# GpSimd takes the six products of C and B, seven column steps move to the front, three PSUM copies change engine, and the order list is new

## The chip, the cores and the metric
The kernel runs on one core of a Trainium2 chip. The metric is the device time of one execution in microseconds (us). The kernel before was timed three times: 318.88, 318.61 and 317.36 us, median 318.61 us. A core has five engines that run side by side, each strictly in its own order: TensorE (PE, with its weight loads shown as PEld), VectorE (DVE), ScalarE (ACT), GpSimd (POOL) and SyncE (SP), which here only issues transfers.

## The reference, cut to what matters
The input x (2048 rows, 640 channels) goes through two branches, and a gate mixes them.

```python
g = sigmoid((x * gate_w).sum(-1, keepdims=True))
# a: per channel d a long convolution with K[d, l], over N = 128 modes
dt = exp(log_dt)[:, None]
logdA, dB = dt * (A_re + 1j*A_im), dt * (B_re + 1j*B_im)
P = exp(logdA[:, :, None] * l)
K = einsum("dn,dnl,dn->dl", C_re + 1j*C_im, P, dB).real
a = irfft(rfft(x, 2L) * rfft(K, 2L))[:L] + x * Dskip
# b: a gated feed-forward block, F = 1728
b = (gelu(x @ w_gate) * (x @ w_up)) @ w_down
return g * a + (1 - g) * b
```

The part that changes is at the start. The product C times B is complex; its real part `vr` = Cre·Bre − Cim·Bim and its imaginary part `vi` = Cre·Bim + Cim·Bre are turned into a size and an angle, from which the tables for K are built.

## The kernel before
Everything is unrolled in Python. The list `ORDER` sets the order of the work: each word is one step, its first letter the kind, digits the indices, and a last letter A or D says whether ScalarE or VectorE does a copy. A planner then places each engine's instructions at compile time by its own reckoning of time, and takes a later step early where the engine would be idle in that reckoning. Chains of dependences keep some of it fixed: `first()` ties VectorE's early steps together in program order, and `table()` does so for most ScalarE steps. Copies of PSUM made by `copy()` (L127 on ScalarE, L131 on VectorE) are in neither chain.

The steps that matter here:
- `a` (`scaled_a`): dt is spread over the partitions by TensorE, ScalarE takes its exponential (`dtb`, L336), VectorE multiplies (`a32`, `b32`, L349 to L351).
- `M` (`early_phases`, L508): VectorE writes phases of the transform matrices. It runs twice.
- `i0` (`columns`, L304 to L319): eleven VectorE steps on columns of one to five elements, in the `first` chain, then seven small GpSimd fills. `i1` makes the flip matrices, `i2` GpSimd's fills (helper L283).
- `x` (`turn_x`): TensorE transposes four or eight 128x128 tiles of x into a PSUM buffer named `cv` (L255), and VectorE (D, L260) or ScalarE (A, L258) copies them to `xT`. `x00` to `x02` make the 640 channels of rows 0 to 511 (c = 0), `x10` to `x12` those of rows 512 to 1023 (c = 1). There are two `cv` buffers, taken in turn, and `x1*` needs the second input transfer.
- `u` (`ffn_up`, L632): ten matmuls of 128x512 into one of two `gu` buffers, gate and up of one feature tile; `pA` or `pD` copies it to `GU` (L127 or L131), `o` sends it to DRAM on SP's queue. There are 56 such steps, and they fill TensorE between other work up to some 165 us. The first four are two of c = 0 and two of c = 1.
- `v` (`phase_and_size`, L439 to L447): the six VectorE products and sums for `vr` and `vi`, 128x640 each, in the `first` chain. Ahead of them stand GpSimd's fill of `zero` and two small GpSimd transfers (`dskc`, `gwc`).
- `S0`, `S1` (`squares` on ScalarE, `sizes` on VectorE), then `r0`, `r1`, `r2`: square root, half angle, angle. `e..` (`exps`, L385) are the exponentials of the tables on ScalarE.
- `t` (`trig`): VectorE writes phases `ph` (L413 and L417, L421), ScalarE takes the sine (L429). `q` (`ktable`, L582 to L590) multiplies the tables on VectorE.
- `!0` (`turn_over(0)`): four GpSimd transfers write `zero` into `GUd` (L913), then the memory of the first stage is given to the tables of `q`.

Of the kernel before, what the change touches and what calls it, by code (L numbers as in the profile page):

```python
# [38 lines left out]
e10 pA u u o e11 e14 t05 y4 pA u t07 u !0 pA pA o pA q05 u u u pA pA o o W o pA o o t02 pA t06 q07 u u q06 y0 t00 pA  # L39
t01 t03 pD o q01 q00 o y1 o o W u pA o q02 q04 u q03 pD t14 o u c02 t10 t16 u pA o c00 pD u C00A c10 pD c01 u !1 pA W  # L40
o o q10 u C01D C02A C10A m u c11 C11D w0 u o pA pA c12 m o u C12A W w1 pA m u pA u o o t11 pA q11 o W u t17 t15 e24 pA
u o pD u o u o pD u pA o W o pD u pD q15 W o e23 pA e22 o u e25 q16 q17 u e20 pD e21 u o o pD o pA t13 o t12 q12 m q14
m u q13 c20 c22 pA C20A u c21 C21D t20 c30 m m c32 !2 pA u C30A t21 C32A c31 m C22A f0 m w2 C31A o t22 q20 F0P t23 U00
U03 U01 V01A w3 V00A q22 q23 pD o U02 h K00 u V03A pA K02 Q00D Q02D o q21 K03 u K01 V02A Q01D Q03A c40 f1 pA C40A o !3
W b00 F1P l00 G00 u L0 c41 C41D pA c42 o l01 C42A l10 g00 b01 w4 f2 U10 b10 b11 P00D U12 P01D V10A u P02D U13 V12A pA
u pA o K10 o K12 Q12A Q10A P03D U11 u G01 K11 V13A pA L1 V11A F2A K13 Q13A Q11A K20 g01 D00 D01 Q20A P10D K22 K21 Q21A
d01A U20 U22 Q22A V20A P11D d00A l11 V22A l20 U23 V23A o K23 D02 f3 Q23A d02D G10 g10 F3A I00 U21 U30 P12D V30A U33
D03 G11 V21A o P20D U31 D10 I10 V33D d10A V31A f4 U32 D11 b20 z00D d03A g11 d11A D13 K30 d13A I01 V32A F4A Q30A K32
Q32A K31 P21D z10A D12 l21 P22D b21 Z00A G20 d12A P23D Q31A l30 Z01A g20 D20 K42 U40 G21 z01A K40 P13D d20D I11 g21
V40A z11A Q40A K41 b30 G30 D21 I20 U42 D23 Q41A K33 d23D K43 d21A Q33A l31 Q43M P30D D22 d22A Z02A Q42A g30 U41 P31D  # L50
b31 D30 V41D I21 G31 V42A U43 z20D V43D d30D g31 z21A P40D D32 P32D P33D d32A I30 z30A D31 J33 j33D d31A D33 J32 d33A
Z03A P41D Z11A P42D J41 J40 j41A P43D j40A j32A Z12A Z10A Z20D J43 J42 j43D Z21D j42A Z22M Z23D Z13D
"""


# [1 line left out]
def kernel(  # L57
# [18 lines left out]
    nc = tc.nc  # L76
    Bsz, L, D = A_u.shape
    N = A_A_re.shape[1]
# [4 lines left out]
    NFULL = F // 128  # L83
    FR = F - 128 * NFULL
    assert 2 * FR == 128
    DP = 128
# [20 lines left out]
    def load_set(x):  # L107
        table(nc.scalar.add_instruction(mybir.InstLoadActFuncSet(
            name=nc.get_next_instruction_name(), engine=mybir.EngineType.Activation, act_func_set_id=x)))

    last_first = [None]
# [164 lines left out]
    def ts(out, in0, s1, s2, op0, op1=None):  # L276
        if op1 is None:
            first(nc.vector.tensor_scalar(out=out, in0=in0, scalar1=s1, scalar2=s2, op0=op0))
        else:
            first(nc.vector.tensor_scalar(out=out, in0=in0, scalar1=s1, scalar2=s2, op0=op0, op1=op1))  # L280

    def fill(out, v):
        nc.gpsimd.memset(out, v)  # L283

    def fills():
        for q, vals in ((0, (3, 1, 3, 1)), (1, (5, 3, 5, 3))):
# [14 lines left out]
            fill(c2[r:r + 1, 6:7], float(c2v))  # L301
        fill(KTt[:, 5], 0.0)

    def columns():  # L304
        first(nc.vector.tensor_copy(out=row[:], in_=par_i[:]))
# [131 lines left out]
    va, vb, vr, vi = (pw.tile([N, D], FP32, name=x) for x in ("va", "vb", "vr", "vi"))  # L437

    def phase_and_size():  # L439
        nc.gpsimd.memset(zero[:], 0.0)  # L440
        nc.gpsimd.dma_start(out=dskc[:], in_=A_Dskip.rearrange("(k p) -> p k", p=128))
        nc.gpsimd.dma_start(out=gwc[:], in_=gate_w.rearrange("(k p) -> p k", p=128))
        for dst, (x0, y0, x1, y1), op in ((vr, (CreT, BreT, CimT, BimT), ALU.subtract),
                                          (vi, (CreT, BimT, CimT, BreT), ALU.add)):
            first(tt(out=va[:], in0=x0[:], in1=y0[:], op=ALU.mult))
            first(tt(out=vb[:], in0=x1[:], in1=y1[:], op=ALU.mult))
            first(tt(out=dst[:], in0=va[:], in1=vb[:], op=op))  # L447

    def squares():
        table(nc.scalar.activation(out=va[:], in_=vr[:], func=ACT.Square))  # L450
# [75 lines left out]

    def early_phases():
        k = 4 + 2 * len(early)
        early.append(phases_of(mats[len(early)], DFT[:, k:k + 2].rearrange("p a r f -> p (a r f)").bitcast(I32)))

    def dft_matrix(mi):
        if mi >= 6:
# [376 lines left out]
    def turn_over(x):  # L909

        if x == 0:
            for c in range(4):
                nc.gpsimd.dma_start(out=GUd[c][FR:128, NFULL], in_=zero[FR:128])  # L913
            ictx.__exit__(None, None, None)
            pools["kq"] = pool(ectx, "kq")
        elif x == 1:
            bctx.__exit__(None, None, None)
            kb4 = pool(kctx, "ktab4", side="right")
            tabs[2] = (kb4.tile([N, 1, NA, DP], BF16, name="eA4"), kb4.tile([N, 1, GP, NB_, 4], BF16, name="eB4"))
        elif x == 2:  # L920
            ectx.__exit__(None, None, None)
            es = pool(ctx, "early")
            pools["mp"] = pool(ctx, "prod")
            pools["kq"] = pool(kctx, "kq4", side="right")
            pools.update(ub=es, pm=es, spec=es)
# [25 lines left out]
    for step in ORDER.split():  # L951
# [5 lines left out]
        if kind == "u" and ups[0][0] < 2:  # L957
            after(*(f"x{ups[0][0]}{i}" for i in range(3)))
        elif kind == "u":
            after(*(f"y{k}" for k in range(KT_)))  # L960
        elif kind == "M":
            assert len(mats) == NMAT + 1 and len(early) < 3
        elif kind == "m":
            after("s", *(("i0", "i2") if len(mats) <= NMAT - 3 else ()), *(("n", "k") if len(mats) <= 5 else ()))
        elif kind in "lb":
            assert not made and all(p[0] != x for p in ups + unsent)
        elif kind == "!" and x == 0:
            assert len(mats) <= NMAT - 1
            after("k", "i0", "i1", "i2", "r2")
# [141 lines left out]
```

## Time and profile before
| | |
|---|---|
| median of three runs | 318.61 us |
| the profiled execution: time | 319.25 us |
| its span | 317.1 us |
| PE busy | 294.0 us (93%) |
| DVE busy | 296.2 us (93%) |
| ACT busy | 246.9 us (78%) |
| POOL busy | 14.2 us (4%) |

The profiled execution took 319.25 us, of which the span from its first to its last record is 317.1 us. The engines' busy times are unions over time: a matmul that overlaps the next counts once. In a timeline row the columns are start, duration (of a whole group where several instructions are merged), engine, line, operation, the tiles as out<-in with shapes, and the count; in square brackets stands how long the engine had been idle before and what ended that. A row of the windows view gives the busy time of each engine in a stretch.

### The profile page before, as it was taken

The numbers are of one execution on the slowest core, as the hardware profiler recorded it, in microseconds if no ns is written. First come the engines' busy times: TensorE is split into PE (matmuls) and PEld (weight loads), VectorE is DVE, ScalarE is ACT, GpSimd is POOL, SyncE is SP. The second block draws the span as 40 slices with busy tenths as digits, with TensorE's granted clock in tenths as the row PEclk, the third lists the DMA queues.
The fourth block names the chain that finished last, engine by engine and source line by source line (L and its number), as shares of the span: only waits on it lengthen the run. The fifth ranks groups of instructions, "written<-read, shape, count | busy, mean of one in ns | idle before, by whom it ended". The sixth has DMA issues, their size and how long they took to land.

```text
span 317.1 us, 6300 instructions
## 1 busy us (share of the span) xinstructions
PE 294.0 (93%) x2463; PEld 182.0 (57%) x2463; DVE 296.2 (93%) x417; ACT 246.9 (78%) x349; POOL 14.2 (4%) x78
## 2 busy tenths in 40 slices
PE   3499999999999999999998879999999999999994
PEld 2344444444555344454476567666686887687773
DVE  4887989999998999999999999989999999999984
ACT  7979999999898999998998667927696737542750
POOL 7720000000000000000000000000000000000000
PEclk9999999999999999999999999999999999999999
DMA  7997456566628885544594699946925352900233
GB/s 214 182 257 193 168 184 207 182 194 216 182 70 178 210 276 179 150 110 128 103 270 151 118 317 236 234 116 168 244 74 165 89 151 63 265 2 0 58 95 83
DMA packets 102543, 51.40 MB, mean 162 GB/s; under 512 B 44081, under 2 KB 95730, under 8 KB 102514
## 3 DMA queue, kind: packets, MB, share of 16 engines
q1 hardware_dynamic: 102256, 50.48, 59.8%
q0 software_dynamic: 256, 0.53, 0.6%
q8 instruction: 19, 0.31, 0.4%
q14 instruction: 10, 0.08, 0.1%
q10 hardware_dynamic: 2, 0.00, 0.0%
HBM read 30.86 MB, written 18.16 MB: 155 GB/s over the span
## 4 chain that ended last, share of the span: by engine, by line
PE 47%; DVE 22%; ACT 14%; DMA 8%; issue 5%; SPq 2%; DVEq 0%; ACTq 0%
PE gu L794 15%; PE gu L632 8%; PE cv L869 6%; DVE ph L413 5%; PE cv L735 4%; PE cv L718 4%; DMA Wd<-in_B_w_down_dram 3%; ACT eA L385 2%; ACT eB L385 2%; PE cv L893 2%; DMA T<-in_A_u_dram 2%; DMA Kd<-Kraw 2%; DVE ph L421 2%; DVE eB L590 1%; DVE sB L589 1%
## 5 line engine op out<-in xcount | busy, mean ns | idle before, releaser
L632 PE MATMUL gu<-xT,W 128*128 128x512 bf16 x540 | 123.7, 383 | 2.8 <-ACT GU L127 1.7
L632 PEld LDWEIGHTS <-W 128*128 128x128 bf16 x540 | 52.3, 99 | 70.1 <-issue 12.5
L794 PE MATMUL gu<-Wd,HT 128*128 128x320 bf16 x448 | 64.4, 299 | 1.1 <-DMA Wd<-in_B_w_down_dram 1.1
L794 PEld LDWEIGHTS <-HT 128*128 128x128 bf16 x448 | 43.5, 98 | 19.2 <-issue 1.3
L429 ACT ACTIVATE T<-ph 128x1024 bf16<-128x1024 int16 (+3 forms) x40 | 46.3, 1196 | 2.6 <-DVE ph L413 1.5
L127 ACT CAST GU<-gu 128x1024 bf16<-128x1024 f32 (+1 forms) x33 | 32.2, 981 | 4.6 <-PE gu L632 3.2
L813 DVE TENSOR_TENSOR Tp<-Uf,Kf 128x6144 bf16<-128x6144 bf16 (+2 forms) x15 | 34.3, 2287 | 0.1
L778 ACT ACTIVATE HT<-HT 128x1792 bf16<-128x1792 bf16 x16 | 26.5, 1692 | 7.0 <-DMA HT<-GUd 5.5
L818 DVE TENSOR_TENSOR Mb<-Mb,Tp 128x4096 bf16<-128x4096 bf16 (+1 forms) x15 | 29.0, 1933 | 0.2
L131 DVE CAST GU<-gu 128x1024 bf16<-128x1024 f32 (+1 forms) x23 | 27.0, 1174 | 0.5 <-PE gu L632 0.5
L735 PE MATMUL cv<-KTt,DFT 128*128 128x128 bf16 x280 | 24.2, 219 | 0.6 <-ACT Uf L127 0.3
L129 ACT ACTIVATE ob<-gu,rat 128x640 bf16<-128x640 f32 x12 | 9.5, 795 | 18.3 <-PE gu L794 18.3
L385 ACT ACTIVATE eB<-a 128x256 bf16<-128x256 f32 (+2 forms) x63 | 23.3, 451 | 0.0
L735 PEld LDWEIGHTS <-DFT 128*128 128x128 bf16 x280 | 21.0, 98 | 1.2 <-issue 0.4
L718 PE MATMUL cv<-pm,DFT 128*128 128x512 bf16 x80 | 20.1, 378 | 1.3 <-DVE Kraw L133 0.6
L127 ACT CAST Uf<-cv 128x1024 bf16<-128x1024 f32 x17 | 16.9, 1019 | 5.2 <-PE cv L718 3.2
L129 ACT ACTIVATE Kf<-cv 128x512 bf16<-128x512 f32 x33 | 17.6, 597 | 3.8 <-PE cv L735 3.7
L413 DVE SCALAR_TENSOR_TENSOR ph<-b,phi 128x256 int32<-128x256 f32 (+1 forms) x63 | 19.6, 385 | 0.0
L869 PEld LDWEIGHTS <-DFT 128*128 128x128 bf16 x320 | 18.8, 98 | 1.3 <-DVE HT L133 0.3
L735 PE MATMUL cv<-KTt,ME 128*128 128x128 bf16 x120 | 18.6, 219 | 0.0
L783 DVE TENSOR_TENSOR HT<-HT,Ut 128x1792 bf16<-128x1792 bf16 x16 | 17.1, 1086 | 0.1
L385 ACT ACTIVATE eA<-a 128x256 bf16<-128x256 f32 (+2 forms) x42 | 15.2, 444 | 0.9 <-DVE a L349 0.9
(182 smaller groups left out, 455.0 us busy)
## 6 DMA issues: line engine op xcount, KB each, us to landing
GUd<-GU SPq DMA_DIRECT2D x52, 256.0 KB, 2.3
HT<-GUd SPq DMA_DIRECT2D x16, 448.0 KB, 4.7
Ut<-GUd SPq DMA_DIRECT2D x16, 448.0 KB, 4.8
W<-in_B_w_gate_dram SPq DMA_DIRECT2D x12, 320.0 KB, 3.5
W<-in_B_w_up_dram SPq DMA_DIRECT2D x12, 320.0 KB, 4.3
fo<-in_A_u_dram SPq DMA_DIRECT2D x20, 128.0 KB, 3.0
out_dram<-GU SPq DMA_DIRECT2D x8, 256.0 KB, 2.6
T<-in_A_u_dram SPq DMA_DIRECT2D x2, 640.0 KB, 7.5
```

The costliest lines, as they stand in the source:

```text
L127: nc.scalar.copy(out=dst, in_=src)
L129: nc.scalar.activation(out=dst, in_=src, func=ACT.Copy, scale=scale)
L385: table(nc.scalar.activation(out=dst, in_=src, func=ACT.Exp, scale=float(scale)))
L413: nc.vector.scalar_tensor_tensor(out=ph[:, x, :], in0=b32[:, dsl], scalar=float(A_OF[x0 + x] + MID), in1=phi[:, dsl], op0=ALU.mult, op1=AL ...
L429: table(nc.scalar.activation(out=dst, in_=phl, func=ACT.Sin, scale=-SIN_SCALE if r and x1 > NA else SIN_SCALE))
L632: nc.tensor.matmul(p[:, r], lhsT=W[:, kt, f0:f0 + 128], rhs=xT[:, kt, 512 * c:512 * (c + 1)], start=(kt == 0), stop=(kt == KT_ - 1))
L718: nc.tensor.matmul(pU[:, ri], lhsT=dmat(e, ri, m), rhs=pm[:, ri, e].rearrange("p c d -> p (c d)"), start=(e == 0), stop=(e == 1))
L735: nc.tensor.matmul(pW[:, ri, 128 * m:128 * (m + 1)], lhsT=lhs, rhs=rhs, start=(first and x == 0 and m == 0), stop=(x == len(seq) - 1), ski ...
L794: nc.tensor.matmul(pD[:, h, 0:DH], lhsT=HT[:, ft, 128 * e:128 * e + 128], rhs=Wd[ft // 7][:, ft % 7, DH * h:DH * (h + 1)], start=(ft == 0) ...
L813: tt(out=dst.rearrange("p c h r f -> p (c h) r f"), in0=U[:, c0:c1].rearrange("p c h f -> p (c h) f")[:, :, None, :].to_broadcast([128, n, ...
L818: tt(out=M, in0=M, in1=T[:, t0:t1], op=ALU.add)
L869: nc.tensor.matmul(pY[:, c % 2, 256 * r + 128 * e:256 * r + 128 * (e + 1)], lhsT=dinv(m, r, e), rhs=pst[part][c // 2][:, c % 2, h[0], h[1] ...
```

## The change
1. `phase_and_size`: the six products and sums go from VectorE to GpSimd. A new helper `pooled()` ties GpSimd's fills, these six and the steps of item 2 together in program order.
2. The fill of `zero` and the transfers of `dskc` and `gwc` move from `v` to `!0`, behind the six products on GpSimd, and the four transfers into `GUd` follow them there.
3. `columns` is cut in two: its first seven VectorE steps become `numbers()` and run in step `a`, ahead of `scaled_a`; four stay in `i0`.
4. `ORDER` is new from its first row on. The same 530 words stand in another sequence, but for six copies that change engine: three `pA` become `pD`, `C22A` becomes `C22D`, `Q00D` becomes `Q00M` (half on each engine), `d02D` becomes `d02A`. The three `p` are the drain of the first `u` step and two more in the second row. `x02D` moves behind `x10D` and `x12A`.
5. `early_phases` may write to another tile when it is called more than three times. It is called twice in both lists, so this does nothing.

```diff
 ORDER = """
-s a M W e04 x01D e02 i2 n M e03 W e00 i0 x00D x02D x10D x12A u e13 e01 pD u pA v o o x11A S0 S1 e05 u u u pD W pD r0 u
-e15 u o pA o u pD pA e12 r1 i1 u pD m o m o u u t04 y3 W u o pD o pD u pD u o pD u r2 u o o W pD o y2 pD o pD u o k o
+s a M W e04 x01D e02 i2 n M e03 W e00 i0 x00D x10D x12A x02D u e13 e01 pD u o pD v o x11A S0 S1 e05 u u u pD W pD u r0
+e15 u o pD o u pD pD e12 r1 m i1 u pD pD u o m o u u t04 y3 W u o o pD o u pD o u pD pD u r2 o o W y2 pD o o k pD u o
...
     def fill(out, v):
-        nc.gpsimd.memset(out, v)
+        pooled(nc.gpsimd.memset(out, v))
...
-    def columns():
+    def numbers():
         first(nc.vector.tensor_copy(out=row[:], in_=par_i[:]))
...
         ts(b16[:], b_i[:], 16.0, None, ALU.mult)
+
+    def columns():
         ts(c2[:, 0:5], c2[:, 0:5], b16[:], None, ALU.add)
...
     def phase_and_size():
-        nc.gpsimd.memset(zero[:], 0.0)
-        nc.gpsimd.dma_start(out=dskc[:], in_=A_Dskip.rearrange("(k p) -> p k", p=128))
-        nc.gpsimd.dma_start(out=gwc[:], in_=gate_w.rearrange("(k p) -> p k", p=128))
         for dst, (x0, y0, x1, y1), op in ((vr, (CreT, BreT, CimT, BimT), ALU.subtract),
                                           (vi, (CreT, BimT, CimT, BreT), ALU.add)):
-            first(tt(out=va[:], in0=x0[:], in1=y0[:], op=ALU.mult))
-            first(tt(out=vb[:], in0=x1[:], in1=y1[:], op=ALU.mult))
-            first(tt(out=dst[:], in0=va[:], in1=vb[:], op=op))
+            pooled(nc.gpsimd.tensor_tensor(out=va[:], in0=x0[:], in1=y0[:], op=ALU.mult))
+            pooled(nc.gpsimd.tensor_tensor(out=vb[:], in0=x1[:], in1=y1[:], op=ALU.mult))
+            pooled(nc.gpsimd.tensor_tensor(out=dst[:], in0=va[:], in1=vb[:], op=op))
...
         if x == 0:
+            pooled(nc.gpsimd.memset(zero[:], 0.0))
+            pooled(nc.gpsimd.dma_start(out=dskc[:], in_=A_Dskip.rearrange("(k p) -> p k", p=128)))
+            pooled(nc.gpsimd.dma_start(out=gwc[:], in_=gate_w.rearrange("(k p) -> p k", p=128)))
             for c in range(4):
-                nc.gpsimd.dma_start(out=GUd[c][FR:128, NFULL], in_=zero[FR:128])
+                pooled(nc.gpsimd.dma_start(out=GUd[c][FR:128, NFULL], in_=zero[FR:128]))
...
         elif kind == "a":
+            numbers()
             scaled_a()
```

The helper that is called:

```python
    def pooled(inst):
        if last_pool[0] is not None:
            tc.add_manual_dep(inst.ins, last_pool[0],
                              mybir.DependencyInfo(mybir.DependencyClass.NoSync, mybir.DependencyReason.DATA),
                              reason="order of the first steps")
        last_pool[0] = inst.ins.name
        return inst
```

More of the change, by code (lines that the diff above doesn't have):

```diff
@@ L36 @@
 ORDER = """
-s a M W e04 x01D e02 i2 n M e03 W e00 i0 x00D x02D x10D x12A u e13 e01 pD u pA v o o x11A S0 S1 e05 u u u pD W pD r0 u
-e15 u o pA o u pD pA e12 r1 i1 u pD m o m o u u t04 y3 W u o pD o pD u pD u o pD u r2 u o o W pD o y2 pD o pD u o k o
-e10 pA u u o e11 e14 t05 y4 pA u t07 u !0 pA pA o pA q05 u u u pA pA o o W o pA o o t02 pA t06 q07 u u q06 y0 t00 pA
-t01 t03 pD o q01 q00 o y1 o o W u pA o q02 q04 u q03 pD t14 o u c02 t10 t16 u pA o c00 pD u C00A c10 pD c01 u !1 pA W
-o o q10 u C01D C02A C10A m u c11 C11D w0 u o pA pA c12 m o u C12A W w1 pA m u pA u o o t11 pA q11 o W u t17 t15 e24 pA
@@ L42 @@
[L42 to L51, printed above, removed]
@@ L52 @@
-Z03A P41D Z11A P42D J41 J40 j41A P43D j40A j32A Z12A Z10A Z20D J43 J42 j43D Z21D j42A Z22M Z23D Z13D
+s a M W e04 x01D e02 i2 n M e03 W e00 i0 x00D x10D x12A x02D u e13 e01 pD u o pD v o x11A S0 S1 e05 u u u pD W pD u r0
+e15 u o pD o u pD pD e12 r1 m i1 u pD pD u o m o u u t04 y3 W u o o pD o u pD o u pD pD u r2 o o W y2 pD o o k pD u o
+e10 pA u u o e11 e14 t05 y4 pA u t07 u u !0 pA q05 t02 u pA o pA u pA pA o o W o pA o o pA t06 q07 u q06 u y0 t00 pA
+t01 t03 q00 q01 pD o o y1 o o u pA o u W q02 q04 q03 pD t14 o u t16 c02 pA o t10 u c00 pD u C00A c10 pD c01 u pA !1 W
@@ new lines @@
+o o C01D q10 u C02A C10A m u c11 C11D w0 u o pA pA c12 m o u C12A w1 W pA m o o u pA u t11 pA q11 o W u t17 u t15 e24
+pA o pD u o u o pD u pA o W o pD u pD u q15 W e23 o pA e21 u o e22 o u e25 q16 q17 e20 pD o pD pA t13 o t12 q12 m q14
+m u o q13 c20 c22 pA c21 C21D C20A u c30 t20 m u C30A m c32 !2 pA t21 C32A c31 C22D f0 m m w2 C31A q20 o t22 F0P t23
+U00 U03 U01 V01A u V03A w3 V00A q22 q23 pD o U02 o h K00 pA K02 Q00M Q02D q21 K03 u K01 V02A Q01D Q03A c40 C40A f1 pA
+o !3 W b00 F1P l00 u L0 c41 G00 C41D pA l01 o c42 C42A l10 g00 b01 P00D w4 f2 b10 b11 P01D U10 V10A u U12 V12A P02D pA
@@ new lines @@
+u pA U13 o K10 o K12 Q12A Q10A P03D G01 u K11 V13A U11 pA L1 V11A F2A K13 Q13A Q11A K20 D00 g01 D01 Q20A P10D K22 U20
+U22 Q22A V20A d01A P11D d00A l11 V22A l20 U23 V23A o K23 K21 Q21A D02 f3 Q23A d02A G10 g10 F3A I00 U21 U30 V30A P12D
+U33 o D03 d03A G11 V21A P20D U31 D10 I10 V33D d10A V31A z00D f4 b20 U32 D11 g11 d11A D13 K30 d13A I01 V32A z10A F4A
+Q30A K32 Q32A K31 P21D D12 l21 P22D b21 Z00A G20 d12A P23D Q31A l30 Z01A g20 D20 K42 U40 G21 z01A P13D K40 d20D I11
+z11A Q40A g21 K41 V40A b30 G30 D21 I20 U42 D23 Q41A K33 d23D K43 d21A Q33A l31 Q43M D22 P30D d22A Z02A Q42A g30 U41
@@ L53 @@
+b31 P31D D30 V41D I21 U43 V42A V43D d30D G31 z20D g31 z21A P40D D32 P32D P33D d32A I30 z30A D31 J33 j33D d31A D33 d33A
+J32 Z03A P41D Z11A J41 J40 j41A P42D P43D j40A j32A Z12A Z10A Z20D J43 J42 j43D Z21D j42A Z22M Z23D Z13D
 """
@@ L109, in load_set @@
             name=nc.get_next_instruction_name(), engine=mybir.EngineType.Activation, act_func_set_id=x)))
+    last_pool = [None]
+    def pooled(inst):
+        if last_pool[0] is not None:
+            tc.add_manual_dep(inst.ins, last_pool[0],
+                              mybir.DependencyInfo(mybir.DependencyClass.NoSync, mybir.DependencyReason.DATA),
+                              reason="order of the first steps")
+        last_pool[0] = inst.ins.name
+        return inst
     last_first = [None]
@@ L528, in early_phases @@
         k = 4 + 2 * len(early)
-        early.append(phases_of(mats[len(early)], DFT[:, k:k + 2].rearrange("p a r f -> p (a r f)").bitcast(I32)))
+        if k < NMAT:
+            t = DFT[:, k:k + 2].rearrange("p a r f -> p (a r f)").bitcast(I32)
+        else:
+            t = kw.tile([N, 2, CW * DP], BF16, name="T", bufs=NT)
+            t = t[:].rearrange("p r x -> p (r x)").bitcast(I32)
+        early.append(phases_of(mats[len(early)], t))
     def dft_matrix(mi):
@@ L961 @@
         elif kind == "M":
-            assert len(mats) == NMAT + 1 and len(early) < 3
+            assert len(mats) == NMAT + 1 and len(early) < 5
         elif kind == "m":
```

## The prediction
> **What bounds the kernel now.** I read the page first, then the windows view by stage, then the timeline of the first 60 us, where the change is.
>
> ```profile
> span 317.1 us, 6300 instructions
> ...
> PE 294.0 (93%) x2463; PEld 182.0 (57%) x2463; DVE 296.2 (93%) x417; ACT 246.9 (78%) x349; POOL 14.2 (4%) x78
> ```
>
> ```profile
> 0.00:16.00 16.00, 6.31 (x52) 5.24 (x53) 10.43 (x36) 13.78 (x28) 11.86 (x67) 1.00 0.92 199
> 16.00:60.00 44.00, 42.62 (x198) 19.03 (x197) 38.88 (x53) 41.65 (x75) 1.96 (x10) 1.00 0.73 205
> 24.00:60.00 36.00, 34.84 (x163) 15.49 (x162) 32.29 (x45) 35.85 (x63) 0.00 (x0) 1.00 0.63 195
> 60.00:300.00 240.00, 232.88 (x2080) 148.20 (x2079) 235.32 (x304) 185.77 (x236) 0.35 (x2) 1.00 0.58 156
> 300.00:317.10 17.10, 12.18 (x142) 9.51 (x139) 11.52 (x26) 5.73 (x13) 0.00 (x0) 1.00 0.41 103
> ```
>
> After each stretch and its length stand the busy times of PE, PEld, DVE, ACT and POOL. TensorE is idle 9.7 us up to 16 us and 4.9 us behind 300; from 16 to 60 it idles 1.4 and from 60 to 300 7.1 us, 8.5 in 284. VectorE idles 5.1 us from 16 to 60, then 4.7 in 240. ScalarE is full from 24 to 60 us (35.85 of 36) and loose later. The chain of waits, followed back from the end, says who holds the path early on:
>
> ```profile
> 16.49 6.13 PE gu L632 x20
> 22.65 1.01 ACT GU L127
> ...
> 45.75 5.92 ACT eB L385 x12
> ...
> 58.93 1.23 DVE sB L589
> ```
>
> It runs through TensorE's first `u` steps and then on ScalarE, and joins VectorE at 58.93. So the end can come earlier mainly by three things: TensorE starts its `u` steps sooner, ScalarE lets go sooner, and VectorE has less to do in front of its full stretch.
>
> **The start of `u`.**
>
> ```profile
> 9.67 1.93 DVE L508 TENSOR_SCALAR DFT<-fr_i,tcol 128x256 int32<-128x256 int32 x4
> 11.52 0.14 DVE L305 CAST row<-par_i 128x1 f32<-128x1 int32 x1
> ...
> 11.64 0.28 DVE L417 TENSOR_SCALAR ph<-b 128x256 int32<-128x256 f32 x1
> ...
> 12.04 0.10 PEld L255 LDWEIGHTS <-T 128*128 128x128 bf16 x1 [1.92 <-DMA T<-in_A_u_dram]
> ...
> 12.50 0.14 DVE L278 TENSOR_SCALAR b<-b_i 128x1 f32<-128x1 int32 x1
> ...
> 12.89 0.68 DVE L421 TENSOR_SCALAR ph<-ph 128x1024 int32<-128x1024 int16 x1
> ...
> 13.62 0.73 DVE L496 TENSOR_SCALAR ph<-fr_i,row 16x512 int32<-16x512 int32 x1
> ...
> 14.33 1.00 DVE L260 COPY xT<-cv 128x1024 bf16<-128x1024 bf16 x2
> ...
> 15.05 1.44 PE L255 MATMUL cv<-ident,T 128*128 128x128 bf16 x12 [4.67 <-DVE xT L260]
> ...
> 16.29 6.33 PE L632 MATMUL gu<-xT,W 128*128 128x512 bf16 x20
> ```
>
> The second input half is in SBUF at 12.04, but the 12 transposes of `x10` and `x12` wait until 15.05, since both `cv` buffers are held: VectorE copies `x00` and `x02` only at 14.33, behind the columns and behind phases that the planner let in between. The first `u` starts at 16.29, right behind those transposes on TensorE.
>
> In the change the seven number steps (11.52 to 12.64, by their first and last rows) go to the front. There VectorE waits anyway:
>
> ```profile
> 5.23 0.83 DVE L349 TENSOR_TENSOR a<-gu,dtb 128x640 f32<-128x640 f32 x1 [2.82 <-ACT dtb L336]
> ```
>
> Seven steps of 0.14 are at most 0.98 us in that hole of 2.82, so they cost nothing; without the hole it would be this 0.98. `x02` also goes behind `x10` and `x12`, so `x10` takes the buffer that is already free (`x01`'s) and its eight transposes can start at 12.04, at 1.44/12 = 0.12 each: done at 13.0. If `x00` is copied by then, `x12`'s four follow to 13.5. VectorE copies `x10` (half to two thirds of the 1.00 of two copies, 0.6) to 13.7, the four of `x02` run to 14.2, and `u` can start at about **14.4: 1.9 us earlier**. The bounds: if all phases (four of 0.28, 0.68, 0.73) stay ahead of `x00`, only the seven steps' own time goes: 12.64 − 11.52, less the three phases of 0.28 between them, is 0.3. Then `x00` is copied from 14.0 to 14.6, `x10` to 15.2, `x02` is transposed by 15.7, and 0.6 is won. The best case, bounded by the transfer, is 2.1. I take 1.9, since only a few of those phases can fit beside four column steps.
>
> **The products.**
>
> ```profile
> 16.71 0.82 DVE L445 TENSOR_TENSOR va<-CreT,BreT 128x640 f32<-128x640 bf16 x1
> ...
> 20.49 1.23 DVE L131 CAST GU<-gu 128x1024 bf16<-128x1024 f32 x1 [0.51 <-PE gu L632]
> ...
> 22.48 0.82 DVE L447 TENSOR_TENSOR vi<-va,vb 128x640 f32<-128x640 f32 x1
> ```
>
> VectorE loses 6 x 0.82 = 4.9 us. It gains three copies of 1.23 = 3.7 us. With the seven steps moved into the hole its load in front of 60 us falls by 1.2 + 0.3 = **1.5 us**; the three later changes of copies (one to VectorE, one and a half away) I count as zero.
>
> What a product costs on GpSimd no row shows. The nearest rows:
>
> ```profile
> 1.50 0.28 POOL masks.py:199 TENSOR_SCALAR_AFFINE_SELECT ident<-ident 128x128 bf16<-128x128 bf16 x1
> ...
> 6.98 0.64 POOL L283 MEMSET KTt<- 128x640 bf16 x1
> ...
> 9.70 0.96 POOL L440 MEMSET zero<- 128x1024 bf16 x1
> ...
> 15.35 2.15 POOL L913 DMA_DIRECT2D GUd<-zero  x4
> 17.50 0.41 POOL L283 MEMSET c<- 1x1 f32 x5
> ```
>
> Below, a step that only writes 640 elements: 0.64. Above, two reads and one write at that rate: 1.92. The row that also reads and writes, 0.28 for 128 elements, gives 5 x 0.28 = 1.4, and I take **1.4**. The Trainium skill, GPSIMD Engine Reference, section "Performance versus the Vector engine", has 4497 ns for a two-input add of 2048 elements; an estimate from that page is 1.41 us here.
>
> ```profile
> L208 SPq DMA_TRANSPOSE BimT<-in_A_B_im_dram x1: 1270/1270/1270, 11.8 to 11.8; - x1
> ...
> DMA to landing us min/median/max: 3.0/3.0/3.0
> ```
>
> The last input is there at 11.8 + 3.0 = 14.8. The first product can be done by then (the seven fills of `i0`, 0.41 and some more, now stand ahead of it and wait for VectorE's columns, about 12.5). Five more take 5 x 1.4 = 7.0: `vi` is ready at **21.8**, with the bounds 18.0 and 24.4. VectorE had it at 22.48 + 0.82 = 23.3. Behind the products on GpSimd wait the fill of `zero` and the six transfers, which took from 9.70 to 17.50 with pauses, 7.8 us: issued by 29.6 in the change. The memory they hold is wanted by the first table product, so they are covered by the time up to its start, and would cost what they came after it:
>
> ```profile
> 48.36 1.20 DVE L589 TENSOR_TENSOR sB<-T,eB 128x2048 bf16<-128x2048 bf16 x1
> ```
>
> **ScalarE.**
>
> ```profile
> 22.65 1.01 ACT L127 CAST GU<-gu 128x1024 bf16<-128x1024 f32 x1 [1.92 <-PE gu L632]
> 23.56 1.02 ACT L258 COPY xT<-cv 128x1024 bf16<-128x1024 bf16 x1
> 24.46 0.75 ACT L450 ACTIVATE va<-vr 128x640 f32<-128x640 f32 x1
> ...
> 32.27 0.99 ACT L127 CAST GU<-gu 128x1024 bf16<-128x1024 f32 x1
> ...
> 35.67 1.01 ACT L127 CAST GU<-gu 128x1024 bf16<-128x1024 f32 x1
> ...
> 41.31 1.99 ACT L429 ACTIVATE T<-ph 128x1024 bf16<-128x1024 int16 x2
> ```
>
> At 22.65 ScalarE has waited 1.92 for a `gu` to copy. That copy is gone, so the copy of `x11` follows the exponentials as soon as TensorE has transposed it, behind the first two `u`: near 21, done near 22. The squares start at about 22.0 instead of 24.46, 2.4 earlier, just behind `vi` at 21.8. The two other copies (0.99, 1.01) go as well: 4.4 us at the sines of 41.31, if VectorE follows.
>
> **The sum.** Up to 60 us ScalarE gains up to 4.4, VectorE at least 1.5 plus what it saves of its 5.1 us of idle time, TensorE 1.9 plus some of its 1.4. Behind 60 us TensorE and VectorE are both full, so the end moves by the least of the three: 1.9 of TensorE's start and, of its 1.4 of idle time, 0.3, since less of it waits for copies. The rest of the list is the same work in another order; it can win at most TensorE's 7.1 of idle time and can lose as much as one wait like the 1.9 above. I take 0, and plus or minus 2 for the range. 319.25 − 2.2 = 317.05; the profiled execution lies 0.64 above the median of 318.61, so the forecast is **316.4 us**.
>
> **Rivals.**
> 1. *The whole of ScalarE's gain arrives* (4.4): for it speaks that ScalarE holds the path up to 58.93; against it that TensorE would have to lose 2.5 more idle time than it starts earlier, of its 8.5. 319.25 − 4.4 − 0.64 = 314.2 us. Chance 0.10.
> 2. *VectorE is held by GpSimd.* If a VectorE step that reads SBUF must wait for the GpSimd product under way, up to 1.4 each, two such holds from 13 to 15 us (the phases of 0.28, 0.68 and 0.73 are of this sort) put the copies of `x10` and `x02` back by up to 2.8 and `u` to 17.2. VectorE's freed time and ScalarE's copies remain, so nothing is won or lost beyond 0.9: 317.7 to 319.5 us, 318.3 as its middle. For it: the phases sit in that very stretch. Against it: the `x` and `GU` copies read PSUM. Chance 0.17. The Trainium skill, SBUF — State Buffer, section "Who interferes with whom", states such an exclusive lock for VectorE steps with two SBUF inputs or in a 2-port mode; no row of before has both engines in such steps at once.
> 3. *Slower: GpSimd's products become ScalarE's wait.* The squares stand in ScalarE's fixed order with the exponentials of `e05` and `e15` behind them, so if `vi` is late, they all wait, and VectorE behind them for its tables. At 3.0 a product (twice my value, or held up by VectorE) `vi` comes at 14.8 + 15.0 = 29.8, the squares 5.3 later than 24.46; the two copies give back 2.0: plus 3.3, 321.9 us. It decides from 24.46 + 2.0 = 26.5 for `vi`, that is 2.3 us a product. For it: POOL rows are rough and none has two inputs. Against it: three times the write-only row is 1.92. Chance 0.25, with a badly placed wait of the new list that costs the same included.
> 4. *The planner doesn't bring `u` forward* (phases stay ahead of `x00`): 0.6 won, 318.0 us. Chance 0.08.
>
> **The numbers.** The forecast holds 0.40. Three runs tell 0.5%, that is 1.6 us, from no change. Faster (below 317.0): the forecast, most of it, and rival 1, with a part of rivals 2 and 4: 0.52. Slower (above 320.2): rival 3 and a part of 2: 0.28. The same: 0.20. The range: 312.5 (rival 1 with the list's 2 us on top) to 322.0 (rival 3). The forecast's own range is 314.4 to 318.0.
>
> **What would show it.** In the profile after: `u` first at about 14.4, not 16.29; no number steps between 11 and 13 us on VectorE; six POOL rows of about 1.4 with the last ending near 21.8; the squares near 22.0 and no wait of 1.92 ahead of them; the first sine of the tables 2 to 4 us before 41.31; from 60 us on the same steps some 2 us earlier. Wrong would be: squares with a wait for GpSimd in front of them, VectorE steps of the early stretch longer than before or with a GpSimd releaser, or a new idle stretch on TensorE behind 60 us.

## The result and the profile after

| | before | changed |
|---|---|---|
| median of ten runs | 317.88 us (317.36 to 318.88) | 316.34 us (315.42 to 317.42) |
| ratio, with its 95% interval | | 0.9955 (0.9939 to 0.997) |
| the profiled execution: time | 319.25 us | 317.27 us |
| its span | 317.1 us | 315.2 us |

With seven more runs the median of before is 317.88, not 318.61. By the ratio the change gains 0.45% of it, 1.4 us (1.0 to 1.9); by the two profiled executions 2.0 us. Both profiled executions are among the slower ones of their kernel (319.25 and 317.27 us), so sizes are taken from the ratio and not from the profiles. The page of the changed kernel, and the windows view in the stretches used before (after each stretch and its length the busy time of PE, PEld, DVE, ACT and POOL):

```profile
span 315.2 us, 6298 instructions
...
PE 294.3 (93%) x2463; PEld 182.2 (58%) x2463; DVE 295.4 (94%) x413; ACT 244.9 (78%) x347; POOL 23.7 (8%) x84
```

```profile
0.00:16.00 16.00, 9.73 (x62) 6.57 (x63) 12.18 (x37) 13.74 (x28) 12.31 (x71) 1.00 0.95 226
16.00:24.00 8.00, 7.33 (x39) 3.41 (x38) 3.16 (x4) 6.93 (x16) 7.76 (x7) 1.00 1.06 224
16.00:60.00 44.00, 41.36 (x195) 18.32 (x194) 37.97 (x54) 41.72 (x75) 11.04 (x12) 1.00 0.73 204
24.00:60.00 36.00, 34.04 (x158) 14.90 (x157) 34.82 (x51) 34.79 (x61) 3.27 (x6) 1.00 0.66 199
60.00:300.00 240.00, 232.97 (x2091) 149.22 (x2090) 235.66 (x301) 184.89 (x236) 0.36 (x2) 1.00 0.58 156
```

TensorE has 3.4 us more busy time behind it at 16 us (9.73 against 6.31). From 16 to 60 it gives 1.3 back: its idle time grows from 1.38 to 2.64. From 60 to 300 nothing changes (7.0 idle against 7.1). That leaves 2.2, of which the longer busy time takes 0.3. Busy time is not the same as work here: the first matmuls of `u` start 0.43 us apart and the later ones 0.22, though the granted clock reads 1.00 in both stretches. The weight loads show it; in the profile of before the pace changes at 20.08, in the changed kernel at 16.37:

```profile
19.70 0.15 PEld L632 LDWEIGHTS <-W 128*128 128x128 bf16 x1 [0.27 <-issue]
...
20.08 2.04 PEld L632 LDWEIGHTS <-W 128*128 128x128 bf16 x10 [0.23 <-issue]
```

The first twenty matmuls of `u` end at 22.62 before and at 19.18 after, so by matmuls the lead is 3.4 us as well. VectorE, which was idle 3.7 of the 36 us from 24 to 60, is now idle 1.2.

The timeline of the changed kernel, with the steps that the prediction costed (start, duration, engine, line, operation; in brackets the idle time before it and what ended that):

```profile
5.26 0.82 DVE L362 TENSOR_TENSOR a<-gu,dtb 128x640 f32<-128x640 f32 x1 [2.07 <-ACT dtb L349]
...
10.89 0.88 PEld L266 LDWEIGHTS <-T 128*128 128x128 bf16 x9 [2.45 <-DMA T<-in_A_u_dram]
...
11.42 1.27 DVE L271 COPY xT<-cv 128x1024 bf16<-128x1024 bf16 x2
...
12.53 1.06 PE L647 MATMUL gu<-xT,W 128*128 128x512 bf16 x2
...
12.76 1.59 POOL L455 TENSOR_TENSOR va<-CreT,BreT 128x640 f32<-128x640 bf16 x1 [0.89 <-DMA BreT<-in_A_B_re_dram]
...
13.13 1.78 DVE L434 TENSOR_SCALAR ph<-ph 128x1024 int32<-128x1024 int16 x1
...
14.32 1.84 POOL L456 TENSOR_TENSOR vb<-CimT,BimT 128x640 f32<-128x640 bf16 x1
...
14.83 0.41 DVE L271 COPY xT<-cv 128x512 bf16<-128x512 bf16 x1
...
15.16 1.27 DVE L506 TENSOR_SCALAR ph<-fr_i,row 16x512 int32<-16x512 int32 x1
...
17.92 2.52 DVE L142 CAST GU<-gu 128x1024 bf16<-128x1024 f32 x2 [1.48 <-PE gu L647]
17.93 1.41 POOL L455 TENSOR_TENSOR va<-CreT,BimT 128x640 f32<-128x640 bf16 x1
...
20.77 1.54 POOL L457 TENSOR_TENSOR vi<-va,vb 128x640 f32<-128x640 f32 x1
...
22.34 0.74 ACT L460 ACTIVATE va<-vr 128x640 f32<-128x640 f32 x1 [1.07 <-POOL vi L457]
...
25.74 8.89 PE L647 MATMUL gu<-xT,W 128*128 128x512 bf16 x40 [0.81 <-DVE GU L142]
...
34.15 1.23 DVE L142 CAST GU<-gu 128x1024 bf16<-128x1024 f32 x1 [1.02 <-DMA GUd<-GU]
...
35.43 2.32 PE L647 MATMUL gu<-xT,W 128*128 128x512 bf16 x10 [0.80 <-DVE GU L142]
...
37.46 1.99 ACT L442 ACTIVATE T<-ph 128x1024 bf16<-128x1024 int16 x2
...
48.97 1.21 DVE L604 TENSOR_TENSOR sB<-T,eB 128x2048 bf16<-128x2048 bf16 x1
```

The seven number steps stand from 2.36 to 3.23 in VectorE's first hole, which shrinks from 2.82 to 2.07, and `a` starts at 5.26 against 5.23: they cost nothing there, as predicted. The copies of `x00` and `x10` start at 11.42, where `x00` was copied at 14.33 before. The first matmuls of `u` stand at 12.53 instead of 16.29, the first drain at 17.92 instead of 20.49, the squares at 22.34 instead of 24.46, the first sines of the tables at 37.46 instead of 41.31. But the first table product on VectorE comes at 48.97, later than its 48.36 before: what ScalarE wins, VectorE, now full, doesn't pass on at once. And TensorE waits for VectorE's copies (0.81, 0.80), one of which itself waits 1.02 for a `GU` buffer that is still being sent.

### The profile page after: what moved, and what is told of

Its sections match the earlier page's. It is cut to its first block, busy times and chain, and to the rows that moved or that the text cites. A ratio compares the mean times of both kernels' runs of the same rounds, so it can differ in the third digit from the quotient of the medians.

```text
span 315.2 us, 6298 instructions
## 1 busy us (share of the span) xinstructions
PE 294.3 (93%) x2463; PEld 182.2 (58%) x2463; DVE 295.4 (94%) x413; ACT 244.9 (78%) x347; POOL 23.7 (8%) x84
## 4 chain that ended last, share of the span: by engine, by line
PE 41%; DVE 21%; ACT 14%; DMA 10%; issue 6%; SPq 3%; POOL 3%; DVEq 0%; ACTq 0%; POOLq 0%
PE gu L809 15%; PE gu L647 8%; PE cv L884 6%; DMA GUd<-GU 4%; ACT GU L138 3%; PE cv L750 3%; ACT T L442 3%; DMA Wd<-in_B_w_down_dram 3%; DVE GU L142 3%; DVE ph L426 3%; PE cv L733 3%; PE cv L908 2%; ACT Uf L138 2%; DMA BreT<-in_A_B_re_dram 2%; DMA Kd<-Kraw 2%
## 5 line engine op out<-in xcount | busy, mean ns | idle before, releaser
L138 ACT CAST GU<-gu 128x1024 bf16<-128x1024 f32 (+1 forms) x30 | 29.3, 981 | 5.5 <-PE gu L647 5.2
L142 DVE CAST GU<-gu 128x1024 bf16<-128x1024 f32 (+1 forms) x26 | 30.5, 1172 | 2.6 <-PE gu L647 1.5
L793 ACT ACTIVATE HT<-HT 128x1792 bf16<-128x1792 bf16 x16 | 26.5, 1692 | 7.4 <-DMA HT<-GUd 7.2
L140 ACT ACTIVATE ob<-gu,rat 128x640 bf16<-128x640 f32 x13 | 10.3, 796 | 18.3 <-PE gu L809 18.3
L434 DVE TENSOR_SCALAR ph<-ph 128x1024 int32<-128x1024 int16 (+3 forms) x20 | 16.4, 818 | 0.2
```

The source lines that it names most:

```text
L138: nc.scalar.copy(out=dst, in_=src)
L140: nc.scalar.activation(out=dst, in_=src, func=ACT.Copy, scale=scale)
L142: nc.vector.tensor_copy(out=dst, in_=src)
```

## The experiments

All ran in five rounds beside the kernel before, in three groups, each group on one chip: e6 seven times, e10 eight, the others twelve times. A ratio compares a run with the kernel before of its own group; the medians of different groups are not compared. Sizes in us below are ratios times 317.88.

| run | what it is | median, us | ratio to before (95%) |
|---|---|---|---|
| the change | | 316.34 | 0.9955 (0.9939 to 0.997) |
| e1 | new list, old code | 318.03 | 1.0004 (0.9989 to 1.0019) |
| e2 | new code, old list | 318.48 | 1.002 (1.0006 to 1.0033) |
| e3 | change, products on VectorE | 316.64 | 0.9971 (0.9953 to 0.9989) |
| e4 | change, number steps back | 317.45 | 0.9997 (0.998 to 1.0013) |
| e5 | before, again | 318.1 | 1.0 (0.9981 to 1.0019) |
| e6 | change, `x02` first | 316.01 | 0.9941 (0.9919 to 0.9963) |
| e7 | change, three copies back | 318.28 | 1.0025 (1.0011 to 1.0039) |
| e8 | new list's first 100 words, then the old | 317.15 | 0.9968 (0.9946 to 0.999) |
| e9 | before, number steps and copies only | 318.01 | 0.9979 (0.9956 to 1.0002) |
| e10 | new code, old list, three copies | 316.48 | 0.996 (0.9931 to 0.999) |
| e11 | e6, third copy back | 319.84 | 1.0054 (1.0035 to 1.0073) |
| e12 | e6, products split | 317.21 | 0.997 (0.9946 to 0.9995) |

The theory after the result (A): the gain is the earlier start of `u`, by `x02`'s place and the number steps. Its rivals: (B) the time that GpSimd frees on VectorE and ScalarE, (C) the rest of the new list.

**e1, the list alone.** The file of before, with only `ORDER` replaced.

```diff
-s a M W e04 x01D e02 i2 n M e03 W e00 i0 x00D x02D x10D x12A u e13 e01 pD u pA v o o x11A S0 S1 e05 u u u pD W pD r0 u
+s a M W e04 x01D e02 i2 n M e03 W e00 i0 x00D x10D x12A x02D u e13 e01 pD u o pD v o x11A S0 S1 e05 u u u pD W pD u r0
...
```

> The new list with the old code: products on VectorE, number steps in i0, zero and the small transfers in v. Theory A (the gain is the earlier start of u, which comes from x02 standing behind x10 and x12 and from the number steps): u starts near 14, as the list alone brings most of it; the six products (4.9 us) then fill VectorE's idle time of 16 to 24 us (8 minus 3.16 busy after the change), so 316.5 to 317.2 us. Theory B (the gain is VectorE's and ScalarE's time, freed by GpSimd): nothing is left of it, 317.9 us or more.

1.0004: nothing. `u` still comes at 15.11, held as before by the columns (`x00` is copied at 14.01). The list already holds the three copies on VectorE, so these alone bring nothing either. Theory A expected half of the gain or more here, and falls in this form.

**e2, the code alone.** The changed file with the old `ORDER` (the diff above, reversed).

> The new code (products on GpSimd, number steps first) with the old list. Theory A: x02 still holds the buffer that x10 wants, so the 12 transposes stand ahead of u again; only the number steps help: u near 15 to 15.5, 317.2 to 317.7 us. Theory B: VectorE has 4.9 us less and the three copies as well, so at least as good as the whole change, 316.3 us or less. Theory C (the gain is in the rest of the list): 317.9 us.

1.002, slower than before, though TensorE starts `u` early, and above all three expectations; theory C's 317.9 is the nearest. Timeline of e2, the first `u`, and VectorE near 100 us:

```profile
13.36 6.12 PE L647 MATMUL gu<-xT,W 128*128 128x512 bf16 x20
```

```profile
96.38 0.83 DVE L434 TENSOR_SCALAR ph<-ph 128x1280 int32<-128x1280 int16 x1 [0.48 <-ACT DFT L554]
98.58 1.09 DVE L144 TENSOR_SCALAR Kraw<-cv,ksign 128x840 bf16<-128x840 f32 x1 [0.57 <-PE cv L623]
101.49 0.96 DVE L598 TENSOR_TENSOR Q<-T,eA 128x1536 bf16<-128x1536 bf16 x1 [1.81 <-PE cv L623]
```

`u` starts 2.9 us earlier than before, without `x02`'s new place, and it is worth nothing: VectorE stands still 2.9 us in all between 96 and 102, 0.5 of it for ScalarE and the rest for TensorE. The changed kernel has no wait there, and the kernel before has a shorter one:

```profile
101.37 0.96 DVE L583 TENSOR_TENSOR Q<-T,eA 128x1536 bf16<-128x1536 bf16 x1 [0.91 <-PE cv L608]
```

So neither A nor B alone makes the gain: A's early start is here, and B's freed time too.

**e3, the products back on VectorE.**

```diff
-            pooled(nc.gpsimd.tensor_tensor(out=va[:], in0=x0[:], in1=y0[:], op=ALU.mult))
+            first(tt(out=va[:], in0=x0[:], in1=y0[:], op=ALU.mult))
...
```

> The changed kernel with the six products on VectorE again, all else kept. Theory A: u starts at 12 to 14 as in the changed kernel, VectorE takes the products in its idle time up to 24 us: 316.3 to 316.8 us. Theory B: 4.9 us more on VectorE ahead of a full stretch, 318 us or more.

0.9971 against 0.9955 for the whole change, so GpSimd's part is some 0.5 us, less than the two intervals can tell from nothing. The order of TensorE and of ScalarE is the same in both programs, instruction for instruction, and those of VectorE and GpSimd differ by the six products alone, so nothing else is mixed in. Theory B, which asked for 318 or more, falls.

**e4, the number steps back in `i0`.**

```diff
-            numbers()
             scaled_a()
...
     def columns():
+        numbers()
```

> The changed kernel with the seven number steps in i0 again. Theory A: x00 and x10 are copied later by 0.4 to 1.0 us and u starts that much later, 316.7 to 317.2 us. Theory B: 316.3 us, as the steps are not on ScalarE's way.

0.9997: the whole gain is gone with seven steps of 0.14 us. The timeline of e4:

```profile
12.21 1.08 POOL L294 MEMSET c<- 1x1 f32 x3 [1.58 <-DVE c L289]
...
13.25 1.27 DVE L271 COPY xT<-cv 128x1024 bf16<-128x1024 bf16 x2
13.78 1.40 POOL L456 TENSOR_TENSOR va<-CreT,BreT 128x640 f32<-128x640 bf16 x1
...
19.29 1.23 DVE L142 CAST GU<-gu 128x1024 bf16<-128x1024 f32 x1 [3.42 <-PE gu L648]
```

The copies of `x00` and `x10` start at 13.25 instead of 11.42, since the planner fills the gaps of that chain with phases; TensorE, though its input was there early in this execution (10.33), has its first `u` drained at 19.29, against 17.92. ScalarE's order is that of the changed kernel here too; its sines come at 38.11, 0.65 later. Theory A's number, 0.4 to 1.0 us, was short of the 1.3 us by the ratios. The two profiles don't show these 1.3 us down to the end: of the 1.4 at the first drain 0.6 is left at the tenth, and the two profiled executions took 317.43 and 317.27. So that the steps cost the gain is shown by the ratios; that they do it through the first drain is likely and not shown.

e1 and e3 are a second test of these steps, with the products on VectorE: beside the number steps they differ only in GpSimd's order and in the place of `zero` and the small transfers. 1.0004 against 0.9971 is 1.0 us. So early number steps win 1.0 us with the products on VectorE and 1.3 with them on GpSimd, and the products, without the early steps, nothing (e1 against e4).

**e5, the kernel before again.** No edit.

> The kernel before, unchanged, for a second profile of it. In the changed kernel's profile the two input transfers of x landed 1.15 us earlier than in that of before (weights first loaded at 6.82 and 10.89 against 7.98 and 12.04), although they were issued at the same times. If that is chance from one execution to the next, this profile has them anywhere from 6.8 to 8.0 and the time is 317.9 us; if it belongs to the program, they land at 8.0 and 12.0 again.

1.0, as it must be, and a second profile:

```profile
7.75 2.14 PEld L255 LDWEIGHTS <-T 128*128 128x128 bf16 x20 [2.53 <-DMA T<-in_A_u_dram]
```

```profile
11.79 0.10 PEld L255 LDWEIGHTS <-T 128*128 128x128 bf16 x1 [1.91 <-DMA T<-in_A_u_dram]
```

The transfers of x land at 7.75 and 11.79. In the profiles of the variants the first lands anywhere from 6.25 (e4) to 7.82 (e8), though the same transfers are issued ahead of it. So the 1.1 us by which they were early in the changed kernel's profile is most likely chance. e3 has the changed kernel's order on TensorE and a landing at 7.79, and its `u` starts at 13.12; by some 0.6 us, then, the profile flatters the start of `u`. The squares of this second profile stand at 23.06 and its span is 315.4, which shows how far one execution of the same program lies from another.

**e6, `x02` first.**

```diff
-s a M W e04 x01D e02 i2 n M e03 W e00 i0 x00D x10D x12A x02D u e13 e01 pD u o pD v o x11A S0 S1 e05 u u u pD W pD u r0
+s a M W e04 x01D e02 i2 n M e03 W e00 i0 x00D x02D x10D x12A u e13 e01 pD u o pD v o x11A S0 S1 e05 u u u pD W pD u r0
```

> The changed kernel with x02 ahead of x10 and x12 in the list, as before. Theory A: the 12 transposes stand ahead of u again, u near 14.5 to 15.5 instead of 12.5 to 13.8, 316.9 to 317.4 us. Theory B: 316.3 us.

0.9941, if anything better; theory A's number is missed. Timeline of e6:

```profile
11.40 1.00 DVE L271 COPY xT<-cv 128x1024 bf16<-128x1024 bf16 x2
...
13.79 6.21 PE L647 MATMUL gu<-xT,W 128*128 128x512 bf16 x19 [0.22 <-issue]
```

With the columns out of the way `x00` and `x02` are copied together at 11.40; the 12 transposes stand ahead of `u` again, but early. The record of `u`'s first matmul is missing here; by its weight load it starts at 13.36, and it runs through, while in the changed kernel it starts at 12.53, stops for `x02`'s transposes and goes on at 13.81. Both have the first drain near 17.9. From 16 to 60 us TensorE idles 1.6 here (42.45 busy of 44), nearly as little as before. So the new place of `x02`, the larger part of the predicted 1.9 us, brings nothing.

**e7, the three copies back on ScalarE.** The second, fifth and seventh `p` of the list; the first of the three drains the second `u` step, not the first one, as the list of changes above has it.

```diff
-... u e13 e01 pD u o pD v o x11A ...
+... u e13 e01 pD u o pA v o x11A ...
-e15 u o pD o u pD pD e12 r1 ...
+e15 u o pA o u pD pA e12 r1 ...
```

> The changed kernel with the three copies of u on ScalarE again. If VectorE's copies are what TensorE gave back between 24 and 40 us (it is idle 1.9 us there, against 0.7 before), TensorE gets this back, and ScalarE's sines come 3 us later: 315.6 to 316.3 us if TensorE decides, 317.0 to 317.9 us if ScalarE does (theory B).

1.0025: 0.7% worse than the change, 2.2 us, the largest part of all, worse than before the change, and above both expectations. The timeline of e7:

```profile
20.25 0.98 ACT L138 CAST GU<-gu 128x1024 bf16<-128x1024 f32 x1
21.15 1.00 ACT L269 COPY xT<-cv 128x1024 bf16<-128x1024 bf16 x1
21.29 0.59 PE L647 MATMUL gu<-xT,W 128*128 128x512 bf16 x2 [1.08 <-ACT GU L138]
```

```profile
97.58 0.90 DVE L430 TENSOR_SCALAR ph<-b 128x256 int32<-128x256 f32 x4 [0.65 <-ACT DFT L554]
100.80 0.96 DVE L598 TENSOR_TENSOR Q<-T,eA 128x1536 bf16<-128x1536 bf16 x1 [1.32 <-PE cv L623]
```

TensorE now waits 1.08 for ScalarE's first copy, which stands behind the exponentials, and the sines come at 39.13. Near 100 us VectorE waits for ScalarE and for TensorE, 2.0 us in all, as in e2; in the changed kernel it doesn't. It is hardly idle time filled early that makes the difference: up to 60 us VectorE idles 9.9 us in the changed kernel and 10.3 in e7. The orders of the engines differ somewhat beyond the copies too (the planner moves VectorE's steps around them), so the 2.2 us are the copies with what the planner makes of them.

**e8, the list's later part.** Words 1 to 100 new, 101 to 530 old.

> The changed kernel with the new list's first 100 words and the old list from there on, which holds the same words but for C22, Q00 and d02. Theories A and B: 316.3 us, since the gain stands in the first 60 us. Theory C (the rest of the list): 317.0 us or more.

0.9968 against 0.9955: no difference that these intervals tell. By the two ratios theory C gets 0.13 of 0.45%, but the intervals are wide enough for nothing or for most of it; the median, 317.15, lies in its range, and the ratio times 317.88, 316.9, between the two expectations. Its profile has the late transfer (first weights at 7.82) and still its `u` begins at 13.13 (by the weight load; the first matmul's record is missing), which settles that most of the earlier start is the program's and not the transfer's.

**e9 and e10, the parts put together.** From e1 to e8 a theory D follows: number steps and copies carry the gain, products add a little, the order of the list nothing. e9 is the kernel before with `numbers()` in `a` and the three copies on VectorE (the second, fifth and seventh, where its expectation says the first); e10 is the changed code with the old list and the three copies.

```diff
-s a M W e04 x01D e02 i2 n M e03 W e00 i0 x00D x02D x10D x12A u e13 e01 pD u pA v o o x11A S0 S1 e05 u u u pD W pD r0 u
-e15 u o pA o u pD pA e12 r1 i1 u pD m o m o u u t04 y3 W u o pD o pD u pD u o pD u r2 u o o W pD o y2 pD o pD u o k o
+s a M W e04 x01D e02 i2 n M e03 W e00 i0 x00D x02D x10D x12A u e13 e01 pD u pD v o o x11A S0 S1 e05 u u u pD W pD r0 u
+e15 u o pD o u pD pD e12 r1 i1 u pD m o m o u u t04 y3 W u o pD o pD u pD u o pD u r2 u o o W pD o y2 pD o pD u o k o
```

> The kernel before with two parts of the change alone: the number steps in step a, and the first, fifth and seventh copy of u on VectorE; old list otherwise, products on VectorE. If these two parts carry the gain (theory D), 316.4 to 317.0 us. If they only pay together with the new sequence of the list, 317.5 us or more.

> The changed kernel's code with the old list, but for the same three copies on VectorE: the two parts of the run before and the products on GpSimd. Theory D: the products add what they added in the whole change (some 0.5 us), 315.9 to 316.7 us. If the new sequence matters: 317.2 us or more.

e10 has 0.996 with three letters of the old list changed: the whole gain, without the new sequence. The same program without these letters is e2, 1.002. e9 has 0.9979, with an interval from 0.9956 to 1.0002: it lies in the middle, at 317.2 us between the two expectations, and the run doesn't decide whether the two parts alone would do. One execution of e9, the profiled one, took 1059.92 us and is left out of the ratio: in it TensorE is busy for 99% of the span, with most of `u`'s matmuls 0.84 us apart throughout, though its granted clock reads 1.00. What made TensorE slow there is not known.

**e11, one copy back.** e6 with the third of the three copies on ScalarE.

```diff
-e15 u o pD o u pD pD e12 r1 ...
+e15 u o pD o u pD pA e12 r1 ...
```

> The changed kernel with x02 first and the third of the three copies on ScalarE again. If TensorE's waits for VectorE's copies between 33 and 38 us cost time, 315.5 to 316.0 us. If ScalarE's way to the sines decides, about 0.7 us more than with all three: 316.5 to 316.9 us.

1.0054, 1.1% worse than e6, far beyond both expectations. The copy stands at 33.07 on ScalarE and puts the sines back by only 0.8 us, to 37.92. The loss comes later:

```profile
99.67 1.09 DVE L144 TENSOR_SCALAR Kraw<-cv,ksign 128x840 bf16<-128x840 f32 x1 [2.96 <-DMA Kd<-Kraw]
101.86 0.96 DVE L598 TENSOR_TENSOR Q<-T,eA 128x1536 bf16<-128x1536 bf16 x1 [1.10 <-PE cv L623]
```

With this one letter the planner puts ScalarE's sines and copies of 55 to 100 us, and with them VectorE's steps, in another order, and VectorE runs into a transfer that isn't there yet (2.96). So this run doesn't measure a copy; it measures how much a changed letter can cost through the planner's order.

**e12, the products split.** e6 with `vr` on GpSimd and `vi` on VectorE.

```diff
+            if dst is vr:
+                pooled(nc.gpsimd.tensor_tensor(out=ta[:], in0=x0[:], in1=y0[:], op=ALU.mult))
...
+            else:
+                first(tt(out=ta[:], in0=x0[:], in1=y0[:], op=ALU.mult))
```

> The changed kernel with x02 first, vr's three products on GpSimd and vi's on VectorE (with two temporaries of its own), in VectorE's idle time of 16 to 24 us. If the squares only wait for vi, they start when x11 is copied, some 0.6 us earlier: 315.4 to 316.0 us. If a VectorE step that reads SBUF waits for the GpSimd product under way, VectorE's products take 1.4 us or more beside GpSimd's instead of 0.82 and nothing is won: 316.0 to 316.8 us.

```profile
13.88 0.87 DVE L460 TENSOR_TENSOR vc<-CreT,BimT 128x640 f32<-128x640 bf16 x1
14.03 1.98 POOL L457 TENSOR_TENSOR vb<-CimT,BimT 128x640 f32<-128x640 bf16 x1
14.67 2.02 DVE L461 TENSOR_TENSOR vd<-CimT,BreT 128x640 f32<-128x640 bf16 x1
16.09 2.01 POOL L458 TENSOR_TENSOR vr<-va,vb 128x640 f32<-128x640 f32 x1
16.61 2.03 DVE L434 TENSOR_SCALAR ph<-ph 128x1024 int32<-128x1024 int16 x1
```

```profile
16.00:24.00 8.00, 5.62 (x28) 2.47 (x27) 6.87 (x7) 8.00 (x20) 7.53 (x9) 0.87 1.08 166
```

The squares start earlier, at 21.15, but the two engines' products run one after the other rather than side by side (2.02 where VectorE takes 0.82 alone, 1.98 and 2.01 where GpSimd takes 1.40 and 1.54), and `u`'s second copy is late by it: TensorE idles 2.38 us from 16 to 24 instead of e6's 0.44. 0.997 against 0.9941; nothing is won, and by its median of 317.21 the run is above both expectations. The granted clock of this stretch is 0.87, against 1.00 in e6, so not all of the loss need come from the two engines.

**Where the differences are made.** One count tells it in all profiles but that of e9, thirteen in number. The fortieth of the 56 copies of `gu` ends at 115.8 and 114.9 us in the two profiles of before, at 114.0 in the changed kernel, 113.3 in e6, 113.2 in e10, 115.9 in e2, 115.2 in e7 and 116.3 in e11. From there to the end every one of them takes 200.4 to 201.4 us, so the list behind it adds nothing that can be told. VectorE's waits near 100 us go with the three bad runs: 2.9 us in e2 against 0.8 in e10, 2.0 in e7 against none in the changed kernel, 4.1 in e11 against none in e6, for losses of 1.9, 2.2 and 3.6 us by the ratios. They are not the whole account: e1 and e4 have no such wait and gain nothing, and what they lose stands elsewhere.

No version was shown to beat the change. e6 is nominally ahead of it, 0.9941 against 0.9955, with intervals that overlap.

## Why the prediction was right, and where it was not

**The time and the sign** came as forecast: 316.34 against 316.4. Part of this is luck: the forecast took 2.2 us off a median of three that stood 0.7 above the later one, and by the ratio 1.4 us were gained. The term that was too large is the last one of the sum: "1.9 of TensorE's start and, of its 1.4 of idle time, 0.3". The start won more than 1.9, and the idle time behind it grew by 1.3 instead of shrinking by 0.3. The prediction also named three things that would show it wrong, and two of them came: squares with a wait for GpSimd in front of them, and VectorE steps of the early stretch longer than before. That the time was right in spite of them is luck too.

**The start of `u`.** Forecast 14.4; measured 12.53 with a break, so about 13.4 in effect (e6's unbroken start, with the same first drain). The cause was put in the wrong place. I let most of it come from `x02` behind `x10`; e6 shows that this brings nothing. It is the number steps, whose leaving I priced at their own time, 0.3 us, and beyond that only as a condition ("If `x00` is copied by then"): they freed the copies of `x00` from 14.33 to 11.42, because several phases of 0.28, 0.68 and 0.73 had stood in the gaps of that chain and most of them moved behind the copies. e4, which undoes this, loses the whole gain, and e1 against e3 shows 1.0 us of it a second time. How soon `u` is drained hangs on chance as well: the same kernel before has its first drain at 20.49 in one profile and at 19.65 in the other.

**The products.** The price was right for the products of bf16 inputs, 1.40 and 1.41 undisturbed; the sum of fp32 inputs took 1.54 with VectorE idle beside it, and beside VectorE's phases the steps took 1.59 to 1.84. `vi` was ready at 22.31 against the forecast 21.8. The squares waited 1.07 for it, so GpSimd was the last to arrive, by half a microsecond more than forecast and far from rival 3's 26.5. The transfers moved behind the products were covered, as said: the last was issued at 27.3, and the first table product came at 48.97.

**VectorE's load.** I counted 4.9 off and 3.7 on and took the balance as VectorE's relief. e3 shows that the 4.9 are worth some 0.5 us, if anything, as VectorE was idle 4.84 of the 8 us from 16 to 24 after the change; with the products there it is busy in that gap. What matters is the other half, the copies (e7: 2.2 us, e10 against e2: 1.9 us, both with what the planner makes of them). As they add to VectorE's load, they can help only by what leaves ScalarE or by the planner's order.

**ScalarE.** Forecast: squares at 22.0 and up to 4.4 at the sines. Measured 22.34 and 3.85. The prediction then let the end follow TensorE alone, "the least of the three"; e2 and e7 show the opposite case, where TensorE starts `u` about as early and the end doesn't move, and VectorE waits 2 to 3 us near 100 us for ScalarE and TensorE. So, as far as these runs tell, the least of the three was the right form, but ScalarE's relief was a condition of the gain and not a surplus.

**Rival 2** happened and didn't decide: the phase step that took 0.68 before took 1.78 beside GpSimd's products, the one of 0.73 took 1.27, and `x02`'s copy came at 14.83. With `x02` first (e6) the same holds fall behind the copies, so they cost nothing there. **Rival 1** didn't arrive; VectorE, idle 1.2 of the 36 us from 24 to 60, had no room to pass ScalarE's 3.85 on. **Rival 4** is nearly e4: 0.9997. That "the rest of the list" counts as zero held within what e10 and e8 can tell.

What stays open: whether number steps and copies alone carry the gain (e9), and whether the copies act by their own time on ScalarE or by the order that the planner makes of them. TensorE's lost 1.3 us from 16 to 60 are nearly back in e6's profile, without a gain that the intervals tell; that the waits for VectorE's copies (0.81 and 0.80) are this loss is read from the profile and was not tried apart from the planner's order.

## What to carry to other kernels

Seven steps of 0.14 us in a chain can hold the path for more than their own time when a planner fills their gaps with long steps; look at what stands between them, not at their sum. When two engines share a load by copies of PSUM, ask which of the two the other engines wait for later, and take the copies off that one early, even if the other is the busier over the whole run; undoing that was the largest single loss here, though part of it may be the planner's order. And a list changed by one letter goes through the planner as a whole: before a difference is put down to the letter, compare the order of the engines in the two programs.

## What the runs showed of the hardware

Some VectorE steps that read SBUF and GpSimd's products held each other up for most of an instruction. The same phase step on VectorE, in e3 (products on VectorE) and in the changed kernel:

```profile
14.36 0.69 DVE L434 TENSOR_SCALAR ph<-ph 128x1024 int32<-128x1024 int16 x1
```

It is 0.69 there, 1.78 beside GpSimd's products, and a product on VectorE went from 0.82 to 2.02 (e12): 1.1 and 1.2 us more, somewhat less than one GpSimd product of 1.40. The copies from PSUM were not longer: 0.41 at 14.83, inside a GpSimd product, against 0.42 in e3. The Trainium skill, SBUF — State Buffer, section "Who interferes with whom", states this lock for VectorE steps with two SBUF inputs or in a 2-port mode; the rows here agree, and the one-input phase step of 1.78 would be of the second sort.

TensorE's pace changes early in the program. `u`'s matmuls start 0.43 us apart at first and 0.22 later, at a granted clock of 1.00 in both. In one profile of before the change comes 3.8 us after the first of them, in the other 1.3 us after, and from the first to the tenth matmul one and the same program took 3.8 and 2.6 us. An earlier start is in part spent at the slow pace.

I had not expected the spread of one and the same transfer: x's first half, always issued among the same transfers, was first read anywhere from 6.25 to 7.98 us, which moves the start of a profile by more than the change gained.
